# Gated linear attention and a bilinear feed-forward layer on one core: weight columns 256 to 768 in four transfers instead of two, GpSimd's scaling of k behind a gate, and products of chunk 1 ahead of chunk 2's last scores

## The chip, the cores and the metric

The kernel runs on one core of a Trainium2 chip. The metric is the device time of one execution in microseconds (us). For the kernel before there are three runs: 195.4, 194.96 and 194.41 us, median 194.96. One further execution, 195.32 us, was profiled; the profile's rows come from it, counted from the start of its span of 193.5 us. Its TensorE clock was granted in full throughout.

## The reference

Two layers stand behind each other. The first is a gated linear attention over 4 batches, 8 heads, 768 steps and a head size of 48; the second multiplies two linear maps of its output and maps the product back:

```python
for t in range(S):
    state = alpha[:, :, t, :, None] * state + einsum('bhd,bhe->bhde', k[:, :, t], v[:, :, t])
    y[:, :, t] = einsum('bhd,bhde->bhe', q[:, :, t], state)
x = y.transpose(0, 2, 1, 3).reshape(B * S, H * D)      # 3072 x 384
out = ((x @ w_a) * (x @ w_b)) @ w_out                  # 384 -> 1536 -> 384
```

All inputs and the output are float32.

## The kernel before

The work is cut into six chunks, 0 to 5. A chunk has two batches (called u = 0 and 1) and 256 steps, which are 512 tokens of the feed-forward layer. Even chunks have batches 0 and 1, odd ones batches 2 and 3; chunks 0 and 1 are the first third of the sequence, 2 and 3 the second, 4 and 5 the last.

The attention of a chunk is done in blocks. The logarithms of alpha (`ln`, ScalarE, L418) are summed along the steps by TensorE (`B`, `A2`, `AQ`), for which VectorE, GpSimd or ScalarE first prepare pairs and the parts of their values (`l2`, `lx`, `H`, `L`, `R`, L426 to L495). The exponentials of the sums (`E`, L539) scale k and q (`mk`, `mq`, VectorE, L550). Before that, the even steps of k and q are scaled by a single step's alpha or its inverse (`lv`, L524, on VectorE or GpSimd, 128x384 each). The scaled values are transposed, in chunks 0 and 1 by TensorE with a copy out of PSUM (`C` L591, `Ce` L597 or L599), later by a DMA transpose that SyncE issues (`T`, L602). Then come the scores (`D`, L672), which are masked on the way out of PSUM (`M` on VectorE, L677) or copied out by ScalarE and masked in place by VectorE (`Mc` L681, `Mm` L685). The output gathers a product with the carried state that crosses blocks (`SB`), one within (`SA`, both L696 or L701) and the product of masked scores and values (`Y`, L696 or L722). The new state is `K` or `KA` on TensorE (L625) and `k` on VectorE (L657 to L661). `X` copies the result out of PSUM (L762, L764), and from chunk 2 on a DMA transpose (`XT`, L769, issued by SyncE) turns it.

The feed-forward layer of a chunk has 12 blocks f of 128 columns of w_a and w_b. `a f w i` and `b f w i` (L784) are three matmuls of 128 rows into PSUM bank i; w is 0 or 1 for one batch (256 tokens) or * for both (512). `as` copies an `a` product into SBUF on ScalarE (L790), where three buffers serve in turn, and `pr` multiplies it on VectorE with the `b` product in PSUM (L798). `o m half i` (L806) is half of an output tile of 128 tokens, six matmuls of 384 columns; `ot` copies it out (L821, L823) and `st` stores it.

PSUM has eight banks. Each operation that writes PSUM names its bank as its last number; scores and `AQ`, `SB` take the named bank and the next one. A bank or a buffer is written again only when its last reader is done, and every wait of this kind is made by semaphores.

The order of all of it is written out by hand in the text PROGRAM (L17 to L265), one operation after the other as `chunk: operation arguments`. Each engine takes the instructions that fall to it in that order and never passes over one that waits. A letter at an operation's end names its engine: V VectorE, P GpSimd, S ScalarE, Y SyncE. DMA issues stand in their engine's order as well: `ld` loads a, q, k or v of a chunk (L411), `W a lo hi` columns lo to hi of w_a (L391, always issued by GpSimd, which turns float32 into bf16 on the way), `Wo` rows of w_out (L394). GpSimd's loads have eight semaphores in turn, so one is issued only when the eighth before it has landed.

The lines of PROGRAM around the change are these (`...` for what is left out):

```
0: W a 256 768; W b 256 768
...
0: SB 1 1; a 2 0 3; a 5 0 6; a 3 0 7; as 3 0; a 4 0 4; as 4 0; as 5 0; b 4 0 0; b 3 0 7
...
2: D 0 0 5; Mc 0 0; Mm 0 0 V; SB 0 1; SA 1; Y 1; X 1 S; XT 1
1: a 4 1 7
```

`gate_t` (L856) is a copy of one element of a transposed tile on GpSimd: GpSimd's later work is behind it, and it waits for the tile.

Of the kernel before, what the change touches and what calls it, by code (L numbers as in the profile page):

```python
# [20 lines left out]
0: cm 1; ld v 1 P; c2 P; c3 P; D 0 1 5; M 0 1; D 0 0 0; SB 0 6; B 1a 4; Bs 1a; Mc 0 0; Mm 0 0 V; B 1b 5; Bs 1b; E 1a i; E 1a b; mq 1a V; mk 1a V; K 0 1 4; E 1b i  # L21
0: v 1 V; mk 1b V; E 1b b; mq 1b V; SA 0; Y 0; X 0 S; dk 1 0; C 1 0 3; Ce 1 0 V; k 0 1 V; b 1 0 6; W a 0 256; de 1; K 1 0 5; k 1 0 V
1: ld a 1 P
0: W a 256 768; W b 256 768
1: ld a 0 P
0: W a 768 1536; C 1 1 1; a 1 0 2; as 1 0; pr 1 0; Ce 1 1 V; W b 768 1536
1: ld q 0 P; ln 1
0: b 0 0 4; a 0 0 2; as 0 0; pr 0 0; D 1 0 6; D 1 1 0; M 1 1
1: ld k 0 P; l2 1 P; ld v 0 P; ld k 1 P
0: Mc 1 0; Mm 1 0 V  # L30
1: H 1 S
0: SB 1 1; a 2 0 3; a 5 0 6; a 3 0 7; as 3 0; a 4 0 4; as 4 0; as 5 0; b 4 0 0; b 3 0 7
1: L 1 V
0: pr 4 0; pr 3 0; SA 1; Y 1; X 1 V; b 2 0 0
1: A2 1 7; ld q 1 P
0: Wo 0 6
2: ld a * P
0: K 1 1 5
1: ln 0
0: as 2 0; pr 2 0  # L40
1: l2 0 V; E 1 b; E 1 i; H 0 S
0: a 3 1 4; a 5 1 2; k 1 1 V; as 3 1; b 3 1 0; a 4 1 1; b 5 0 7; pr 5 0; as 5 1; a 6 * 5; b 5 1 4; a 11 * 3; pr 5 1; pr 3 1; as 4 1; b 4 1 1; pr 4 1
1: L 0 V; dk * 6
0: Wo 6 12; as 11 *; as 6 *
1: ra 0
0: b 6 * 3; pr 6 *; b 11 * 0; pr 11 *
1: A2 0 7; E 0 i; de *
2: ld q * P
1: lv 0 q P; ld v 1 P; lv 0 k V; mk 0 V
0: a 10 * 2; a 7 * 3  # L50
1: E 0 b; mq 0 V
0: as 10 *; a 2 1 4; as 2 1; b 10 * 1; pr 10 *; as 7 *; b 7 * 0; pr 7 *
1: v 0 S; ra 1
0: b 2 1 3; a 0 1 5
1: C 0 0 4
0: a 1 1 6; as 1 1
1: Ce 0 0 S
0: pr 2 1; b 1 1 1; pr 1 1; as 0 1
1: KA 0 02; k 0 0 V; k 0 1 V; C 0 1 7
0: b 0 1 6  # L60
1: Ce 0 1 S
2: ld k * P
1: lv 1 k P
3: ld a * P
0: pr 0 1
1: mk 1 V; lv 1 q P; mq 1 V
0: a 8 * 1; as 8 *; a 9 * 5; as 9 *
2: ld v * P
0: b 8 * 2; pr 8 *
1: D 0 0 6; M 0 0; D 0 1 3; Mc 0 1; SB 0 4  # L70
# [25 lines left out]
1: as 3 0; b 3 0 7; a 1 0 6; as 1 0  # L96
4: ld a * P
1: b 7 0 0; b 1 0 4; pr 1 0; as 7 0; pr 7 0; pr 3 0
2: mk 0 V
1: SB 1 0  # L100
3: ln *
1: a 6 0 2; as 6 0; b 9 0 3; a 4 0 5; a 9 0 6; as 9 0; pr 9 0
2: mq 1 V; T 1
0: o 2 0 4
1: b 4 0 6; b 6 0 7
2: lv 0 q P; mq 0 V
# [162 lines left out]
def kernel(  # L269
# [29 lines left out]
    ld = ctx.enter_context(tc.tile_pool(name="ld", bufs=2))  # L299
# [21 lines left out]
    go = cst.tile([1, 1], F32, name="go")  # L321
# [641 lines left out]
```

## Time and profile before

| | us |
|---|---|
| runs | 195.4, 194.96, 194.41 |
| median | 194.96 |
| profiled execution | 195.32 |
| its span | 193.5 |
| TensorE busy (matmuls) | 184.7 |
| VectorE busy | 138.4 |
| ScalarE busy | 103.3 |
| GpSimd busy | 50.8 |

Engines are named PE (TensorE matmul), PEld (its weight loads, beside the matmuls), DVE (VectorE), ACT (ScalarE), POOL (GpSimd) and SP (SyncE). A row of the timeline has the start and the length in us, the engine, the line of the kernel, the operation, the written and the read tile, their shapes, a count where equal instructions were merged, and in brackets the idle time before it with what ended it. Matmuls overlap, so that a row's length is more than the distance to the next one, and the distance is what a step costs. In the view by slices a digit is the busy share of a fortieth of the span in tenths. A row of the DMA view has the transfer, the queue, the count, the size in SBUF and the time from issue to landing.

### The profile page before, as it was taken

The page shows a single profiled execution, that of the slowest core. Times are in us where ns is not written, and L with a number is a line of the kernel's source. Part 1 is how long each engine was busy: PE and PEld are TensorE (multiplying, and loading weights), DVE is VectorE, ACT ScalarE, POOL GpSimd, SP SyncE. Part 2 cuts the span into 40 slices and gives each one's busy share as a digit, 9 for nine tenths or more (in the row PEclk, how much of TensorE's full clock was granted, in tenths as well). Part 3 has the DMA queues.
Part 4 walks back from the last instruction along what each step waited for, and adds up shares of the span by engine and source line. Part 5 has one row for each costly group of instructions (what it writes and reads, how often), then busy time and mean ns, then how long its engine had stood idle before and what let it go on. Part 6 is the DMA issues. An engine that isn't in the chain of part 4 may idle for free.

```text
span 193.5 us, 5877 instructions
## 1 busy us (share of the span) xinstructions
PE 184.7 (95%) x2509; PEld 111.4 (58%) x2509; DVE 138.4 (71%) x230; ACT 103.3 (53%) x189; POOL 50.8 (26%) x71
## 2 busy tenths in 40 slices
PE   7889699999999998999999999999999999999993
PEld 3467475666687865744556644555544566544462
DVE  4688777999899799597979499875854871156520
ACT  4565575886775676556565235875255622154401
POOL 8999645850640425000400020050000000000000
PEclk9999999999999999999999999999999999999999
DMA  5999999999999999489995488999297005021013
GB/s 139 261 214 211 243 247 251 252 246 260 243 220 231 198 234 219 57 233 213 172 219 69 100 203 178 118 191 120 59 180 160 3 3 122 0 99 67 0 42 122
DMA packets 67162, 30.96 MB, mean 160 GB/s; under 512 B 58064, under 2 KB 65120, under 8 KB 67136
## 3 DMA queue, kind: packets, MB, share of 16 engines
q0 software_dynamic: 18640, 14.16, 41.3%
q1 hardware_dynamic: 48352, 16.34, 39.9%
q8 instruction: 19, 0.31, 0.7%
q10 hardware_dynamic: 144, 0.10, 0.2%
q14 instruction: 7, 0.06, 0.1%
HBM read 25.98 MB, written 4.74 MB: 159 GB/s over the span
## 4 chain that ended last, share of the span: by engine, by line
PE 84%; POOL 6%; DMA 5%; issue 2%; DVE 1%; ACT 0%; POOLq 0%; DVEq 0%
PE psum L784 47%; PE psum L806 24%; DMA wb_t<-in_moe_w_b_dram 5%; PE psum L672 3%; PE psum L722 2%; PE psum L625 2%; PE psum L696 2%; PE psum L701 1%; PE psum L505 1%; PE psum L817 1%; POOL v_t L411 1%; POOL a_t L411 1%; PE psum L591 1%; POOL wa_t L391 1%; DVE prod L798 1%
## 5 line engine op out<-in xcount | busy, mean ns | idle before, releaser
L784 PE MATMUL psum<-xT,wb_t 128*128 128x512 bf16 (+1 forms) x270 | 57.0, 337 | 1.3 <-DMA wb_t<-in_moe_w_b_dram 1.3
L784 PE MATMUL psum<-xT,wa_t 128*128 128x512 bf16 (+1 forms) x270 | 56.1, 337 | 0.0
L806 PE MATMUL psum<-wo_t,prod 128*128 128x384 bf16 x276 | 48.5, 326 | 0.0
L784 PEld LDWEIGHTS <-wb_t 128*128 128x128 bf16 x270 | 25.5, 98 | 21.9 <-DMA wb_t<-in_moe_w_b_dram 1.6
L784 PEld LDWEIGHTS <-wa_t 128*128 128x128 bf16 x270 | 25.6, 98 | 19.7 <-issue 0.2
L806 PEld LDWEIGHTS <-prod 128*128 128x128 bf16 x276 | 26.1, 98 | 17.0
L681 ACT ACTIVATE m<-psum 128x1024 bf16<-128x1024 f32 x16 | 16.3, 1023 | 6.1 <-PE psum L672 5.9
L823 DVE COPY ot<-psum 128x384 f32<-128x384 f32 (+1 forms) x13 | 6.9, 538 | 15.7 <-PE psum L806 13.2
L524 POOL TENSOR_TENSOR q_t<-q_t,ra 128x384 f32<-128x384 f32 x8 | 8.8, 1103 | 34.7 <-DVE prod L798 18.4
L821 ACT ACTIVATE ot<-psum 128x384 f32<-128x384 f32 (+1 forms) x12 | 5.7, 477 | 12.9 <-PE psum L806 11.9
L524 POOL TENSOR_TENSOR k_t<-k_t,a_t 128x384 f32<-128x384 f32 x5 | 6.0, 1197 | 22.8 <-DVE QKp L550 17.9
L685 DVE TENSOR_TENSOR m<-m,mask 128x1024 bf16<-128x1024 bf16 x16 | 11.6, 734 | 0.3 <-ACT m L681 0.2
L418 ACT ACTIVATE la<-a_t 128x1536 f32<-128x1536 f32 (+2 forms) x9 | 9.5, 1053 | 3.7 <-DMA a_t<-in_alpha_dram 3.7
L550 DVE TENSOR_TENSOR QKp<-k_t,invb 128x768 bf16<-128x768 f32 x10 | 11.0, 1105 | 0.2
L677 DVE TENSOR_TENSOR m<-psum,mask 128x1024 bf16<-128x1024 f32 x8 | 9.8, 1219 | 1.6 <-PE psum L672 1.5
L550 DVE TENSOR_TENSOR QKp<-q_t,beta 128x768 bf16<-128x768 f32 x10 | 9.3, 947 | 0.0
L672 PE MATMUL psum<-kqT 64*64 64x128 bf16 x384 | 8.6, 218 | 0.2 <-DVE kqT L599 0.2
L411 POOL DMA_DIRECT2D v_t<-in_v_dram x8 | 8.6, 1075 | 0.6 <-PE psum L784 0.5
L762 ACT ACTIVATE ys<-psum 128x768 bf16<-128x768 f32 x7 | 5.6, 808 | 5.6 <-PE psum L722 3.3
L672 PEld LDWEIGHTS <-kqT 64*64 64x64 bf16 x384 | 6.3, 107 | 2.7 <-issue 2.3
L411 POOL DMA_DIRECT2D a_t<-in_alpha_dram x6 | 6.3, 1043 | 5.6 <-DVE prod L798 2.9
L444 PE MATMUL psum<-wz 128*128 128x512 bf16 x17 | 5.5, 473 | 1.2 <-DVE og L336 1.2
(272 smaller groups left out, 272.0 us busy)
## 6 DMA issues: line engine op xcount, KB each, us to landing
out_dram<-ot SPq DMA_DIRECT2D x23, 192.0 KB, 2.6
a_t<-in_alpha_dram POOLq DMA_DIRECT2D x3, 768.0 KB, 14.2
k_t<-in_k_dram SPq DMA_DIRECT2D x3, 768.0 KB, 6.7
q_t<-in_q_dram POOLq DMA_DIRECT2D x2, 768.0 KB, 12.8
v_t<-in_v_dram POOLq DMA_DIRECT2D x4, 384.0 KB, 9.2
q_t<-in_q_dram SPq DMA_DIRECT2D x2, 768.0 KB, 6.7
a_t<-in_alpha_dram POOLq DMA_DIRECT2D x3, 384.0 KB, 5.7
q_t<-in_q_dram POOLq DMA_DIRECT2D x3, 384.0 KB, 13.1
```

The lines of the kernel that those rows point to most:

```text
L411: eng.dma_start(out=t[:, us, hs].rearrange("p b h r d -> p (b h) (r d)"), in_=src[ch.b0 + us.start:ch.b0 + us.stop, hs, ch.s * 2 * C:(ch.s ...
L418: nc.scalar.activation(out=ch.la[:, us, hs].rearrange("p b h r d -> p (b h r d)"), in_=ch.a[:, us, hs].rearrange("p b h r d -> p (b h r d) ...
L524: eng.tensor_mul(x, x, by)
L550: eng.tensor_mul(QKp[ch.c % 2][:, u, j, :, hs, :D], src[:, u, hs].rearrange("p h r d -> p r h d"), f)
L672: nc.tensor.matmul(s2[g * HC:(g + 1) * HC, r, p, rk, :], lhsT=ch.kqT[u][rs, 1, rk, 2 * h + p, g * HC:(g + 1) * HC], rhs=queriesT(ch, u, 2 ...
L677: nc.vector.tensor_mul(m.rearrange("p r a k s -> p (r a) (k s)"), ch.s2[u, h].rearrange("p r a k s -> p (r a) (k s)"), maskn(4))
L681: nc.scalar.activation(out=m.rearrange("p r a k s -> p (r a) (k s)"), in_=ch.s2[u, h].rearrange("p r a k s -> p (r a) (k s)"), func=AF.Copy)
L685: eng.tensor_mul(x, x, maskn(4))
L784: nc.tensor.matmul(p, lhsT=(wa_t, wb_t)[w][:, kk, f * 128:(f + 1) * 128], rhs=ch.xT[:, us.start // 2:us.stop // 2, kk].rearrange("p u g s ...
L806: nc.tensor.matmul(op, lhsT=ch.prod[:, f, at:at + C], rhs=wo_t[:, f, :], start=(f == 0), stop=(f == NFF - 1))
L821: nc.scalar.activation(out=o_, in_=i_, func=AF.Copy)
L823: eng.tensor_copy(o_, i_)
```

## The change

It has four parts, all but one of them moves of operations in PROGRAM. The number of matmuls and their shapes stay the same.

1. The loads of columns 256 to 768 of w_a and w_b, two transfers of 512 columns each, become four of 256 columns, in the order a, b, a, b. Behind them the products of chunk 0 are put in another order: `b 2` and `b 3` come before `a 4` and `a 5`, and `b 4` and `b 5` behind chunk 0's inner products. `SB 1` stands ahead of the second half of the scores. `H` and `L` come behind the `as` copies. Many PSUM banks are other ones.
2. In chunk 1, GpSimd's scaling `lv 0 q` stands ahead of the load of chunk 2's q instead of behind it, `lv 1 k` and `lv 1 q` ahead of the load of chunk 3's alpha. `a 10` goes ahead of the products that need the last columns of w_b; `a 1 1` ahead of the transposes `C 0 0`; `pr 7` ahead of `pr 10`.
3. In chunk 2, `mq 1` and the transpose `T 1` stand ahead of `mk 0`. Chunk 1's `a 4 1`, `as 4 1` and `o 0 0` stand ahead of chunk 2's last scores `D 0 0`, and `o 0 1` directly behind its `Y 1`; `b 9 1` comes behind `AQ 3`.
4. GpSimd's scaling of chunk 3's k (`lv 0 k`, `lv 1 k`) moves behind a new `gatem 0 0`, a copy of one element of chunk 2's last masked scores.

```diff
-0: W a 256 768; W b 256 768
+0: W a 256 512; W b 256 512; W a 512 768; W b 512 768
...
-0: b 0 0 4; a 0 0 2; as 0 0; pr 0 0; D 1 0 6; D 1 1 0; M 1 1
+0: b 0 0 4; a 0 0 2; as 0 0; pr 0 0; D 1 0 6; SB 1 2; D 1 1 0; M 1 1
...
-1: H 1 S
-0: SB 1 1; a 2 0 3; a 5 0 6; a 3 0 7; as 3 0; a 4 0 4; as 4 0; as 5 0; b 4 0 0; b 3 0 7
-1: L 1 V
-0: pr 4 0; pr 3 0; SA 1; Y 1; X 1 V; b 2 0 0
+0: a 2 0 4; as 2 0; a 3 0 5; as 3 0; b 2 0 6; pr 2 0; b 3 0 0; a 4 0 7; as 4 0; a 5 0 1; as 5 0; pr 3 0
+1: H 1 S; L 1 V
+0: SA 1; Y 1; X 1 V; b 4 0 4; pr 4 0; b 5 0 5; pr 5 0
...
-0: a 3 1 4; a 5 1 2; k 1 1 V; as 3 1; b 3 1 0; a 4 1 1; b 5 0 7; pr 5 0; as 5 1; a 6 * 5; b 5 1 4; a 11 * 3; pr 5 1; pr 3 1; as 4 1; b 4 1 1; pr 4 1
-1: L 0 V; dk * 6
+0: a 3 1 1; a 5 1 2; k 1 1 V; as 3 1; b 3 1 0; a 4 1 3; as 5 1; b 5 1 4; as 4 1; b 4 1 5; pr 3 1; pr 5 1; a 6 * 6; a 11 * 7; pr 4 1
+1: L 0 V; dk * 1
+0: a 10 * 2
...
+1: lv 0 q P
 2: ld q * P
-1: lv 0 q P; ld v 1 P; lv 0 k V; mk 0 V
-0: a 10 * 2; a 7 * 3
+1: ld v 1 P; lv 0 k V; mk 0 V
+0: a 7 * 4
...
-0: as 10 *; a 2 1 4; as 2 1; b 10 * 1; pr 10 *; as 7 *; b 7 * 0; pr 7 *
+0: as 10 *; a 2 1 5; as 2 1; b 10 * 1; as 7 *; b 7 * 0; pr 7 *; pr 10 *
...
-1: KA 0 02; k 0 0 V; k 0 1 V; C 0 1 7
+1: KA 0 02; k 0 0 V; k 0 1 V; C 0 1 1
...
-3: ld a * P
...
+3: ld a * P
-0: a 8 * 1; as 8 *; a 9 * 5; as 9 *
+0: a 8 * 7; as 8 *; a 9 * 5; as 9 *
...
-2: mk 0 V
+2: mq 1 V; T 1
...
-2: mq 1 V; T 1
+2: mk 0 V
...
-3: ra 1; lv 1 q P; ld v * P; lv 0 k P; lv 1 k P
+3: ra 1; lv 1 q P; ld v * P
...
-2: D 0 0 5; Mc 0 0; Mm 0 0 V; SB 0 1; SA 1; Y 1; X 1 S; XT 1
-1: a 4 1 7
+1: a 4 1 5; as 4 1; o 0 0 7
+2: D 0 0 1; Mc 0 0; Mm 0 0 V; gatem 0 0; SB 0 5; SA 1; Y 1; X 1 S; XT 1
+3: lv 0 k P; lv 1 k P
+1: o 0 1 -; ot 0 V
 4: ln *
-1: as 4 1; b 9 1 0; pr 9 1; o 0 0 5
 3: AQ 3
+1: b 9 1 0; pr 9 1
 2: SA 0; Y 0; X 0 S; XT 0
 5: ld a * Y
-1: o 0 1 -; ot 0 V; a 1 1 6; a 10 1 1; as 1 1; as 10 1
+1: a 1 1 1; a 10 1 2; as 1 1; as 10 1
...
+    def gate_m(x, u, h):
+        nc.gpsimd.tensor_copy(go, x.m[int(u), int(h)][0:1, 0, 0, 0, 0:1])
```

More of the change, by code (lines that the diff above doesn't have):

```diff
@@ L37 @@
 2: ld a * P
-0: K 1 1 5
+0: K 1 1 6
 1: ln 0
-0: as 2 0; pr 2 0
 1: l2 0 V; E 1 b; E 1 i; H 0 S
-0: a 3 1 4; a 5 1 2; k 1 1 V; as 3 1; b 3 1 0; a 4 1 1; b 5 0 7; pr 5 0; as 5 1; a 6 * 5; b 5 1 4; a 11 * 3; pr 5 1; pr 3 1; as 4 1; b 4 1 1; pr 4 1
-1: L 0 V; dk * 6
+0: a 3 1 1; a 5 1 2; k 1 1 V; as 3 1; b 3 1 0; a 4 1 3; as 5 1; b 5 1 4; as 4 1; b 4 1 5; pr 3 1; pr 5 1; a 6 * 6; a 11 * 7; pr 4 1
+1: L 0 V; dk * 1
+0: a 10 * 2
 0: Wo 6 12; as 11 *; as 6 *
@@ L47 @@
 1: A2 0 7; E 0 i; de *
+1: lv 0 q P
 2: ld q * P
-1: lv 0 q P; ld v 1 P; lv 0 k V; mk 0 V
-0: a 10 * 2; a 7 * 3
+1: ld v 1 P; lv 0 k V; mk 0 V
+0: a 7 * 4
 1: E 0 b; mq 0 V
-0: as 10 *; a 2 1 4; as 2 1; b 10 * 1; pr 10 *; as 7 *; b 7 * 0; pr 7 *
+0: as 10 *; a 2 1 5; as 2 1; b 10 * 1; as 7 *; b 7 * 0; pr 7 *; pr 10 *
 1: v 0 S; ra 1
-0: b 2 1 3; a 0 1 5
-1: C 0 0 4
-0: a 1 1 6; as 1 1
+0: b 2 1 3; a 0 1 6; a 1 1 4
+1: C 0 0 5
+0: as 1 1
 1: Ce 0 0 S
-0: pr 2 1; b 1 1 1; pr 1 1; as 0 1
-1: KA 0 02; k 0 0 V; k 0 1 V; C 0 1 7
-0: b 0 1 6
+0: pr 2 1; b 1 1 7; pr 1 1; as 0 1
+1: KA 0 02; k 0 0 V; k 0 1 V; C 0 1 1
+0: b 0 1 4
 1: Ce 0 1 S
@@ L127 @@
 2: Mm 1 0 V
-1: o 2 0 7
+1: o 2 0 6
 2: SB 1 3; D 0 1 1; Mc 0 1; Mm 0 1 V; k * 1 V
@@ L133 @@
 1: st 2 Y
-2: D 0 0 5; Mc 0 0; Mm 0 0 V; SB 0 1; SA 1; Y 1; X 1 S; XT 1
-1: a 4 1 7
+1: a 4 1 5; as 4 1; o 0 0 7
+2: D 0 0 1; Mc 0 0; Mm 0 0 V; gatem 0 0; SB 0 5; SA 1; Y 1; X 1 S; XT 1
+3: lv 0 k P; lv 1 k P
+1: o 0 1 -; ot 0 V
 4: ln *
-1: as 4 1; b 9 1 0; pr 9 1; o 0 0 5
 3: AQ 3
+1: b 9 1 0; pr 9 1
 2: SA 0; Y 0; X 0 S; XT 0
 5: ld a * Y
-1: o 0 1 -; ot 0 V; a 1 1 6; a 10 1 1; as 1 1; as 10 1
+1: a 1 1 1; a 10 1 2; as 1 1; as 10 1
 3: E 0 b; E 0 i
-1: b 4 1 2; pr 4 1; b 8 1 5; b 1 1 1; a 8 1 6; b 10 1 0; pr 1 1; o 3 0 2; pr 10 1; as 8 1; pr 8 1; o 3 1 -; ot 3 S; st 3 Y
+1: b 4 1 7; pr 4 1; b 8 1 0; b 1 1 5; a 8 1 6; b 10 1 1; pr 1 1; o 3 0 2; pr 10 1; as 8 1; pr 8 1; o 3 1 -; ot 3 S; st 3 Y
 2: a 4 * 7; as 4 *
@@ L861 @@
         "gatet": gate_t,
+        "gatem": gate_m,
         "c1": lambda x: const_fill(),
```

## The prediction

> **What bounds the kernel now.** I read the page first, then the timeline of TensorE for its waits, and only around these the other engines.
>
> ```profile
> PE 184.7 (95%) x2509; PEld 111.4 (58%) x2509; DVE 138.4 (71%) x230; ACT 103.3 (53%) x189; POOL 50.8 (26%) x71
> DMA  5999999999999999489995488999297005021013
> ```
>
> TensorE is busy 95% of the span, and the DMA engines are full from slice 2 to 16, so to about 78 us. The change leaves every matmul in place, so only idle TensorE time can be won. Its timeline shows two waits of over a microsecond behind the start-up (in brackets: the idle time and what ended it). The first is in chunk 0, with three later points that I use below:
>
> ```profile
> 23.40 0.83 PE L784 MATMUL psum<-xT,wb_t 128*128 128x256 bf16 x6 [1.30 <-DMA wb_t<-in_moe_w_b_dram]
> ...
> 27.91 0.81 PE L784 MATMUL psum<-xT,wa_t 128*128 128x512 bf16 x3
> ...
> 37.59 0.44 PE L625 MATMUL psum<-vx,QKp 64*64 64x48 bf16 x32
> ...
> 40.78 0.64 PE L672 MATMUL psum<-kqT 64*64 64x128 bf16 x32
> ```
>
> At 23.40 `b 4 0` waits for columns 256 to 768 of w_b. 27.91 is `a 6`, the first product that needs columns from 768 on; 37.59 is `KA 0` and 40.78 `D 0 0` of chunk 1. The second wait is in chunk 2:
>
> ```profile
> 71.70 0.42 PE L672 MATMUL psum<-kqT 64*64 64x128 bf16 x16
> ...
> 73.50 0.18 PE L701 MATMUL psum<-S,kqT 64*64 64x48 bf16 x1 [1.26 <-issue]
> ...
> 74.25 0.50 PE L784 MATMUL psum<-xT,wa_t 128*128 128x256 bf16 x3
> ...
> 74.92 1.14 PE L806 MATMUL psum<-wo_t,prod 128*128 128x384 bf16 x6
> ...
> 77.24 1.15 PE L806 MATMUL psum<-wo_t,prod 128*128 128x384 bf16 x6
> ...
> 82.50 1.46 PE L784 MATMUL psum<-xT,wa_t 128*128 128x512 bf16 x6
> ```
>
> These rows are `D 0 0`, `SA 1`, `a 4 1` (with `b 9 1` behind it), `o 0 0`, `o 0 1`, and chunk 2's first product `a 4 *`. The view calls the cause of the 1.26 us "issue"; the VectorE rows show it:
>
> ```profile
> 70.01 0.95 DVE L495 TENSOR_TENSOR lh<-l 128x768 f32<-128x768 f32 x1
> 70.88 0.68 DVE L685 TENSOR_TENSOR m<-m,mask 128x1024 bf16<-128x1024 bf16 x1
> ...
> 72.99 0.56 DVE L661 TENSOR_TENSOR S<-tmp,bl 128x384 bf16<-128x384 f32 x1
> 73.46 1.76 DVE L495 TENSOR_TENSOR ll<-lh 128x768 f32<-128x768 f32 x1
> 75.14 1.49 DVE L685 TENSOR_TENSOR m<-m,mask 128x1024 bf16<-128x1024 bf16 x1
> 73.24 2.84 POOL L524 TENSOR_TENSOR k_t<-k_t,a_t 128x384 f32<-128x384 f32 x2 [4.47 <-DMA k_t<-in_k_dram]
> ```
>
> `SA 1` reads the state that L661 finishes at 73.55. The last row is GpSimd's scaling of chunk 3's k: beside it L495 takes 1.76 us and L685 1.49, where the first two rows, of the same forms, took 0.95 and 0.68.
>
> **Part 1: products ahead of chunk 2's scores.** Two 256-wide products lie between 74.25 and 74.92, so one is 0.33 us. From 77.24 to 82.50 run three halves of `o` and seven products: (5.26 - 7 x 0.33) / 3 = 0.98 for a half. The change puts `a 4 1` and `o 0 0` ahead of `D 0 0`: 0.33 + 0.98 = 1.31 us. `D 0 0` then starts near 73.0, and its own 0.24 and the state products reach the wait at about 73.5, when the state is ready. So the wait is filled, and as nothing but the order changed, everything behind `Y 1` has 1.31 us less ahead of it. The DVE row that releases `SA 1` keeps its place. I count 1.25, the wait itself.
>
> What is late next is chunk 2's transposed activations, `XT 0`, which `a 4 *` needs:
>
> ```profile
> 77.35 0.81 ACT L762 ACTIVATE ys<-psum 128x768 bf16<-128x768 f32 x1 [0.54 <-PE psum L722]
> xT<-ys SPq DMA_TRANSPOSE x8, 3.1
> kqT<-QKp SPq DMA_TRANSPOSE x8, 4.4
> ```
>
> Now the copy ends at 78.16 and the transpose lands 3.1 us on, at 81.3, against 82.50. Changed, `a 4 1` (0.33) no longer lies between `Y 1` and `Y 0`, so the copy ends near 77.8 and the landing is at 80.9, against `a 4 *` at 82.50 - 1.25 = 81.25. It is still covered, by 0.35. At 4.4 us (the median of the other kind of transpose) it would be 82.2, a new wait of 0.95; if it lands sooner, nothing is gained. I take 0, as 3.1 is of the same kind.
>
> The `gatem` copy holds GpSimd until chunk 2's last mask product is done. VectorE's L495 and L685 then run at 0.95 and 0.68, so 1.6 us of VectorE time come free, but `Y 0`, which reads L685's result, stands behind `o 0 1`, the cumulative sums and `b 9 1` anyway: 0. Queued behind the gate on GpSimd are the two scalings of k (at most 1.42 each, done by about 78) and then chunk 4's q; chunk 3's `mk 0`, which waits for them, stands behind `a 4 *`, so after 81. The copy itself is one element. Also 0; were this cover gone, it would be 2.84. Swapping `mq 1` and `mk 0` of chunk 2 lets SP issue its first transpose one product of VectorE (0.95) earlier, ahead of the same queue: 0.
>
> **Part 2: four weight transfers.** The queue is first in, first out, so landing is issue plus the view's last figure. First the GpSimd rows of the issues, then the landings, each with its own issue:
>
> ```profile
> 12.74 0.92 POOL L411 DMA_DIRECT2D a_t<-in_alpha_dram  x1
> 13.65 0.75 POOL L391 DMA_DIRECT2D wa_t<-in_moe_w_a_dram  x1
> 14.38 0.76 POOL L391 DMA_DIRECT2D wb_t<-in_moe_w_b_dram  x1
> ...
> 16.01 0.80 POOL L391 DMA_DIRECT2D wa_t<-in_moe_w_a_dram  x1
> ...
> 18.42 0.92 POOL L411 DMA_DIRECT2D k_t<-in_k_dram  x1
> ```
>
> ```profile
> a_t<-in_alpha_dram POOLq DMA_DIRECT2D x1, 384.0 KB, 5.7
> wa_t<-in_moe_w_a_dram POOLq DMA_DIRECT2D x1, 384.0 KB, 6.6
> wb_t<-in_moe_w_b_dram POOLq DMA_DIRECT2D x1, 384.0 KB, 9.0
> wa_t<-in_moe_w_a_dram POOLq DMA_DIRECT2D x1, 576.0 KB, 11.2
> k_t<-in_k_dram POOLq DMA_DIRECT2D x1, 384.0 KB, 14.7
> ```
>
> So alpha lands at 18.4, w_a's middle at 20.25, w_b's at 23.4, w_a's last part at 27.2, chunk 1's k at 33.1. The two middle transfers take 1.8 and 3.1, together 4.9. Cut in four, b 2 and b 3 have their columns near 20.3, and a 4, a 5 near 21.8. The two issues more (0.76 each) delay GpSimd by 1.5 us, and its `l2 1` behind them, but every load behind them waits 5 us or more in the queue anyway.
>
> How much later the four land as a whole, d, no row shows. A half at the faster transfer's rate is 0.9, at the slower's 1.57; four are 3.6 or 6.3 against 4.9: d between -1.3 and +1.3. I take +0.4: each has rows half as long, which can hardly be quicker, while w_a's last part and the alpha ahead of it, 960 KB from 23.4 to 27.2, or 0.76 per 192 KB, speak for a price by the byte.
>
> The Trainium skill (DMA: Bandwidth & Descriptors, Measured (HBM→SBUF, 128 partitions, SWDGE, issued from GpSimd)) speaks against cutting: batch to 1 MiB; its 0.95 us for 64 KB and 6.15 for 1 MB leave, as an estimate, 0.6 fixed for each transfer. By it d is 1.2 and the sum below 1.0 instead of 1.8.
>
> **What TensorE does with it.** Two more rows, from VectorE's timeline and from the chain of work that ended last:
>
> ```profile
> 20.47 1.23 DVE L677 TENSOR_TENSOR m<-psum,mask 128x1024 bf16<-128x1024 f32 x1 [0.17 <-PE psum L672]
> 24.23 0.95 PE psum L696 x54
> ```
>
> TensorE ran dry at 22.1 (23.40 - 1.30) after four products (`a 2` to `a 5`, 1.32). Now `a 2`, `a 3`, `b 2` come first, 0.33 each. `b 3` writes bank 0, which `M 1 1` (the L677 row) empties at 21.7, and 0.27 later as `SB 1` now stands ahead of its scores: a wait of up to 0.4. Then `b 3`, `a 4`, `a 5` (0.99) and the 54 inner matmuls (0.95) bring it to 23.9, and `b 4` needs 23.4 + 0.4 = 23.8. So 1.30 - 0.4 = 0.9 is in hand. At `a 6` TensorE has 0.66 more behind it (`b 4 1`, `b 5 1`): 27.91 + 0.66 - 0.9 = 27.7, and its columns land at 27.2 + 0.4 = 27.6. But it is not all kept, because chunk 1 hangs on k's landing:
>
> ```profile
> 33.18 0.56 DVE L524 TENSOR_TENSOR k_t<-k_t,a_t 128x384 f32<-128x384 f32 x1
> 33.84 1.57 DVE L550 TENSOR_TENSOR QKp<-k_t,invb 128x768 bf16<-128x768 f32 x1
> 35.33 0.95 DVE L550 TENSOR_TENSOR QKp<-q_t,beta 128x768 bf16<-128x768 f32 x1
> 36.20 0.72 DVE L798 TENSOR_TENSOR prod<-as__705,psum 128x512 bf16<-128x512 bf16 x1
> 33.26 1.33 POOL L524 TENSOR_TENSOR q_t<-q_t,ra 128x384 f32<-128x384 f32 x1
> 37.10 0.38 ACT L790 ACTIVATE as__741<-psum 128x256 bf16<-128x256 f32 x1 [0.82 <-PE psum L784]
> 39.59 0.60 ACT L790 ACTIVATE as__812<-psum 128x512 bf16<-128x512 f32 x1
> ```
>
> L524 starts as k lands. GpSimd's q scaling, which stretches `mk 0` to 1.57, moves ahead of a load that GpSimd issues, to about 32 to 33, so `mk 0` takes 0.95. With d = 0.4: k at 33.5, then about 0.55 + 0.9 + 0.9 to 35.85, then `pr 7` and `pr 10` at 0.62 each, now in this order, to 37.1. `KA 0`, released by `pr 7`, starts at 36.5 instead of 37.59. But `as 1 1` takes the buffer that `pr 10` gives back, so ScalarE's row at 37.10 stays there, and so its chain to the row at 39.59 (`as 8`, done 40.2). `a 8` now sits in bank 7, which `D 0 0` needs: 40.2 instead of 40.78. The head is worth 0.55: with d = +1.3 it is a loss of 0.35; with d = -1.3 the products' own time caps it, I estimate at the 1.1 that `KA 0` wins.
>
> **The sum.** 1.25 + 0.55 = 1.8 us. The profiled execution took 195.32, its span 193.5 and 1.8 around it, so its span should be 191.7. That execution is 0.36 above the median of the runs, 194.96; from the median the time is 193.2, and with the bounds of d alone, 0.9 to 2.35 less, 192.6 to 194.1.
>
> **The rivals.** First, the landings eat the head (d of 1 or more): only 1.25 less something is left, 193.7 to 194.1. The full DMA slices speak for it, the price by the byte against it. The skill's page says the same, in d = 1.2. Chance 0.17.
>
> Second, the wait moves to `XT`: at 4.4 us, 0.95 goes back, 194.1 to 194.2. For it speaks that only 0.35 covers it; against, that DMA traffic falls off in just these slices. 0.10.
>
> Third, the order doesn't do what it says: the state at 73.55 comes later as well, since VectorE's row waits for a mask on ScalarE, or the head's stalls only move. Nothing in the rows delays it; 195.0. 0.06.
>
> Fourth, the slower end: a transfer's price goes by the piece. Four at the mean of the two, 2.47, are 9.9 against 4.9, d = 4.9: k lands at 38.0, `D 0 0` comes at 44.7, 3.9 late, and with 1.25 won 2.7 are lost: 197.7. It decides against the change from d = 2.2 on. The 0.76 per 192 KB speaks against it. 0.12.
>
> **How the numbers follow.** The forecast holds 0.55. Within 0.5% (about what a measurement of this kernel can tell from no change) is 194.0 to 195.9. Faster: 0.53 of the forecast, 0.10 of the first rival, 0.02 of the second: 0.65. Slower: the fourth and a little else, 0.13. The rest, 0.22, is the same. The range, 192.2 to 195.1, takes the forecast with 0.4 of scatter below it, the three middle rivals, and leaves out the fourth.
>
> **What would show it.** Right: no wait for wb_t near 23, or one under 0.4; `SA 1` without its 1.26; L495 near 0.95 and the following L685 near 0.68; w_a's last part landing by 28; `a 4 *` about 1.8 us earlier. Wrong: w_a's last part landing after 28.5, a new wait at `a 6` or `D 0 0` of chunk 1 above 1 us, or TensorE waiting at `a 4 *` for the transpose.

## The result, and the profile after

| | before | after |
|---|---|---|
| median of 8 runs, us | 195.23 | 196.82 |
| lowest to highest | 194.41 to 195.64 | 195.69 to 198.33 |
| profiled execution | 195.32 | 196.17 |
| its span | 193.5 | 194.4 |

The ratio of the two times is 1.0077, with a 95% interval of 1.0051 to 1.0103: the changed kernel is slower by 0.8%. Here and below, ratios are estimated from the runs outside a slower state of the chip, and are not exactly the quotients of the medians, which have all runs. The line numbers of the helpers are two further down than before, and in the experiments up to six.

First comes the timeline of TensorE after the change, at the places that the prediction spoke of (start, length, engine, line, operation, tiles, shape, count, and the idle time before it with what ended it):

```profile
16.08 0.43 PE L627 MATMUL psum<-vx,QKp 64*64 64x48 bf16 x16 [0.76 <-ACT prod L541]
...
23.33 0.49 PE L786 MATMUL psum<-xT,wb_t 128*128 128x256 bf16 x3 [0.23 <-DVE m L679]
...
40.77 0.64 PE L674 MATMUL psum<-kqT 64*64 64x128 bf16 x32
...
67.49 0.64 PE L674 MATMUL psum<-kqT 64*64 64x128 bf16 x32 [0.46 <-DMA kqT<-QKp]
...
77.58 0.50 PE L786 MATMUL psum<-xT,wa_t 128*128 128x256 bf16 x3
79.39 0.50 PE L786 MATMUL psum<-xT,wa_t 128*128 128x256 bf16 x3 [1.31 <-issue]
...
83.31 1.46 PE L786 MATMUL psum<-xT,wa_t 128*128 128x512 bf16 x6
```

The wait for w_b's columns at 23.4 is gone, and so are the 1.26 us at `SA 1`. But `D 0 0` of chunk 1 stands at 40.77, where it was before (40.78), `D 1 1` of chunk 2 at 67.49 instead of 66.97 (its row of before is the one below), behind a wait for `T 1` that was not there, and `a 10 1` at 79.39 behind a new wait of 1.31. `a 4 *` comes at 83.31, 0.81 later than before, and this distance stays to the end: the spans differ by 0.9.

```profile
66.97 0.64 PE L672 MATMUL psum<-kqT 64*64 64x128 bf16 x32
```

Part of the lost start belongs to this one execution. Its clock row on the page, and the row of before for the first line above:

```profile
PEclk9969999999999999999999999999999999999999
```

```profile
14.49 0.43 PE L625 MATMUL psum<-vx,QKp 64*64 64x48 bf16 x16 [0.58 <-ACT prod L539]
```

The third slice, from 9.7 to 14.6 us, was granted 0.6 of the clock, and TensorE was 1.6 us behind at 16 us, ahead of anything that the change touches; before had the full clock throughout. The other runs after were nearly all at full clock and not faster, so the dip is not why the kernel is slower; it hides what the head would have shown here.

The late `D 1 1` has its counterpart in SyncE's queue. Its timeline (SPq: issues of DMA), after and then before:

```profile
57.50 0.54 SPq L841 DMA_DIRECT2D out_dram<-ot  x1
58.95 8.32 SPq L604 DMA_TRANSPOSE kqT<-QKp  x2
```

```profile
57.55 0.53 SPq L839 DMA_DIRECT2D out_dram<-ot  x1
60.15 6.08 SPq L602 DMA_TRANSPOSE kqT<-QKp  x2
```

`T 1` and `T 0` of chunk 2 were issued 1.2 us earlier, and the issue took 2.2 us longer. By its semaphore `T 1` landed at 67.44 instead of 65.97: **issued earlier, landed later.**

VectorE and GpSimd did what was forecast:

```profile
73.98 0.95 DVE L497 TENSOR_TENSOR ll<-lh 128x768 f32<-128x768 f32 x1
75.04 0.69 DVE L687 TENSOR_TENSOR m<-m,mask 128x1024 bf16<-128x1024 bf16 x1
```

```profile
75.96 1.96 POOL L526 TENSOR_TENSOR k_t<-k_t,a_t 128x384 f32<-128x384 f32 x2
```

With the scaling behind the gate, L497 takes 0.95 instead of 1.76 and L687 0.69 instead of 1.49. And the transfers, from GpSimd's issues and from the DMA view (last figure: median from issue to landing):

```profile
17.83 0.74 POOL L393 DMA_DIRECT2D wa_t<-in_moe_w_a_dram  x1
```

```profile
wb_t<-in_moe_w_b_dram POOLq DMA_DIRECT2D x3, 192.0 KB, 6.2
wa_t<-in_moe_w_a_dram POOLq DMA_DIRECT2D x1, 576.0 KB, 9.7
```

w_a's last part lands at 17.83 + 9.7 = 27.5, against 27.2 before, and chunk 1's k by its semaphore at 33.43 against 33.09: what stands behind the four transfers comes 0.3 to 0.4 us later, about as assumed. The four themselves land, by their semaphores, at 19.36, 20.34, 21.33 and 22.39, so the last of them is even 1.0 ahead of w_b's transfer before (23.35); the alpha behind them lands at 25.03 instead of 24.61. In another run with the four transfers, e1 below, they land at 19.69, 21.11, 23.16 and 23.71, so the time of a single one scatters.

**What "issue" is.** The instruction that stops at 79.39, `a 10 1`'s first weight load, has no semaphore to wait for, and neither had the product of `SA 1` that stopped before; each only follows the products ahead of it. The page shows one queue that the prediction passed over:

```profile
q8 instruction: 19, 0.31, 0.7%
```

These are 19 packets, 0.31 MB, so 16 KB each, spread over the whole span: TensorE's own code on its way to it. They serve 5018 weight loads and matmuls (2509 each on the page), one packet for some 264. Counting TensorE's instructions in the trace in order of their start (its few semaphore instructions too), the stop at `SA 1` before stands behind number 2241 and the one at `a 10 1` after behind number 2497: exactly 256 apart, or 64 bytes of a packet for each. And the stop ends 1.64 us after the end of such a packet (70.70 to 71.86, stop over at 73.50), after the change 1.48 us (76.98 to 77.91, over at 79.39). So theory CODE was that TensorE runs into a block of 256 instructions that has not come yet; where hundreds of short matmuls follow each other, it uses a block up faster than the next one comes.

### The profile page after: what moved, and what is told of

Its sections match the earlier page's. It is cut to its first block, busy times and chain, and to the rows that moved or that the text cites. A ratio compares the mean times of both kernels' runs of the same rounds, so it can differ in the third digit from the quotient of the medians.

```text
span 194.4 us, 5878 instructions
## 1 busy us (share of the span) xinstructions
PE 185.7 (96%) x2509; PEld 112.6 (58%) x2509; DVE 135.8 (70%) x230; ACT 103.2 (53%) x189; POOL 51.7 (27%) x74
## 4 chain that ended last, share of the span: by engine, by line
PE 86%; DMA 7%; DVE 2%; SPq 1%; issue 1%; ACT 1%; DVEq 0%
PE psum L786 45%; PE psum L808 23%; DMA kqT<-QKp 4%; PE psum L674 3%; DMA k_t<-in_k_dram 2%; PE psum L627 2%; PE psum L724 2%; PE psum L698 2%; PE psum L593 2%; PE psum L703 1%; PE psum L507 1%; SPq L413 1%; PE psum L819 1%; PE psum L573 1%; PE psum L462 1%
## 5 line engine op out<-in xcount | busy, mean ns | idle before, releaser
L687 DVE TENSOR_TENSOR m<-m,mask 128x1024 bf16<-128x1024 bf16 x16 | 10.8, 686 | 0.4 <-ACT m L683 0.3
L526 POOL TENSOR_TENSOR k_t<-k_t,a_t 128x384 f32<-128x384 f32 x5 | 5.4, 1085 | 18.4 <-DVE QKp L552 17.5
L552 DVE TENSOR_TENSOR QKp<-q_t,beta 128x768 bf16<-128x768 f32 x10 | 9.8, 988 | 0.0
L552 DVE TENSOR_TENSOR QKp<-k_t,invb 128x768 bf16<-128x768 f32 x10 | 9.5, 951 | 0.2
L674 PE MATMUL psum<-kqT 64*64 64x128 bf16 x384 | 9.2, 226 | 0.5 <-DMA kqT<-QKp 0.5
```

Source lines behind the costliest of these rows:

```text
L526: eng.tensor_mul(x, x, by)
L552: eng.tensor_mul(QKp[ch.c % 2][:, u, j, :, hs, :D], src[:, u, hs].rearrange("p h r d -> p r h d"), f)
L674: nc.tensor.matmul(s2[g * HC:(g + 1) * HC, r, p, rk, :], lhsT=ch.kqT[u][rs, 1, rk, 2 * h + p, g * HC:(g + 1) * HC], rhs=queriesT(ch, u, 2 ...
L687: eng.tensor_mul(x, x, maskn(4))
```

## The experiments

Names of theories: CODE as above. TRANSPOSE: the swap of `mq 1; T 1` with `mk 0` makes `T 1` late, and that is the loss. HEAD: the four transfers cost the time. Each ratio is against the kernel before, measured beside it on the same chip (medians 195.4 to 195.5, and 195.23 for the first comparison), with its 95% interval.

### The parts one by one

Four kernels: the new head alone (parts 1 and 2 of the change), the swap alone, the new order in chunk 2 with the gate alone, and the changed kernel without the swap.

```diff
 e1: before +
-0: W a 256 768; W b 256 768
+0: W a 256 512; W b 256 512; W a 512 768; W b 512 768
...
 e2: before +
+2: mq 1 V; T 1
...
-2: mq 1 V; T 1
+2: mk 0 V
 e3: before +
+1: a 4 1 5; as 4 1; o 0 0 7
+2: D 0 0 1; Mc 0 0; Mm 0 0 V; gatem 0 0; SB 0 5; SA 1; Y 1; X 1 S; XT 1
...
 e4: after, with the lines of e2 undone
```

> The kernel before with the change's first part alone (the four weight transfers and the new order of products in chunk 0); chunk 2's order is the old one. Theory CODE (TensorE stops where it reaches a stretch of 256 of its instructions that has not been fetched yet; the change only moved that stop from `SA 1` to `a 10 1`) and theory TRANSPOSE (the earlier `T 1` lands later, `D 1 1` of chunk 2 waits for it): both say that the head does nothing, as chunk 1's `KA 0` and `D 0 0` started at the same times in both profiles: within 0.4 us of the kernel before, the 1.26 us stop at `SA 1` still there. Theory HEAD (the loss comes from the four transfers): slower by 0.8 us or more, with `D 0 0` of chunk 1 after 41.3.

> The kernel before with one move alone: `mq 1; T 1` ahead of `mk 0` in chunk 2. TRANSPOSE: `T 1` is issued about 1.2 us earlier and lands 1 to 1.5 us later, `D 1 1` starts 0.5 us later, the time is 0.4 to 0.8 us more. CODE: a later `D 1 1` comes ahead of the stop at `SA 1`, whose end is set by the fetch and not by TensorE, so 0 to 0.3 us more and a shorter stop. My prediction's own step said 0.

> The kernel before with the last part alone: `a 4 1`, `o 0 0` ahead of chunk 2's `D 0 0`, the GpSimd gate, no swap, old head. CODE: no stop at `SA 1`, one of 1.2 to 1.6 us 256 instructions later, before `a 10 1`; `a 4 *` within 0.4 us of the kernel before, and so is the time. TRANSPOSE and HEAD: the wait at `SA 1` is filled and stays filled, 1.0 to 1.25 us less.

> The changed kernel with the swap undone (`mk 0` ahead of `mq 1; T 1` again), all else as changed. TRANSPOSE: it wins back 0.5 to 1.6 us against the changed kernel and comes out at or below the kernel before. CODE: the stop before `a 10 1` stays at 1.2 to 1.9 us; at most 0.5 us is won back against the changed kernel. HEAD: still 0.8 us or more slower than before.

| | median, us | ratio to before |
|---|---|---|
| e1, head alone | 194.59 | 0.9962 (0.9944 to 0.9981) |
| e2, swap alone | 195.79 | 1.0019 (0.9991 to 1.0047) |
| e3, order and gate alone | 195.60 | 1.0006 (0.9983 to 1.0028) |
| e4, after without swap | 195.30 | 1.0017 (0.9989 to 1.0046) |
| after | 196.82 | 1.0077 (1.0051 to 1.0103) |

HEAD falls: the head wins 0.4%, where CODE and TRANSPOSE had expected nothing and HEAD a loss. One row of e1's TensorE shows it, `D 0 0` of chunk 1 at 40.22 instead of 40.78:

```profile
40.22 0.64 PE L672 MATMUL psum<-kqT 64*64 64x128 bf16 x32
```

The order in chunk 2, which was to win 1.25 us, wins nothing, and its stop is where CODE put it. From the timelines of e3, then of e4:

```profile
78.13 0.60 PE L786 MATMUL psum<-xT,wa_t 128*128 128x256 bf16 x4 [0.69 <-issue]
...
82.32 1.47 PE L786 MATMUL psum<-xT,wa_t 128*128 128x512 bf16 x6
```

```profile
78.54 0.50 PE L786 MATMUL psum<-xT,wa_t 128*128 128x256 bf16 x3 [1.28 <-issue]
...
82.47 1.46 PE L786 MATMUL psum<-xT,wa_t 128*128 128x512 bf16 x6
```

In both `SA 1` does not wait, `a 10 1` does, and `a 4 *` is at 82.3 and 82.5 as before (82.50). In e1 and e2, where the order is the old one, the stops stand at the same two counts, 2241 and 2497, in other shares (e1: none and 0.76, although the one at `SA 1` was expected to stay; e2: 0.48 and 1.08), since the fetch comes earlier or later in every run. The swap alone costs nothing that can be told, and yet the changed kernel is 0.6% above e4 by their ratios (1.5 us by the medians). That is what TRANSPOSE had expected of e4; CODE had allowed 0.5 us at most. The parts do not add up, and the next runs look for the reason.

### Moving the boundaries

The same work, with more TensorE instructions ahead of it: the warm-up products at the start, whose result nobody reads, are cut into pieces of 64 columns. Every boundary of 256 then falls on another instruction. From the profile before, the time that TensorE needs for each block of 256 at any shift is read off as the distance of two starts, less the stops.

```diff
 e5: before +                      (16 instructions more)
-fill 7 2
+fill 6 2; fine 9 2
 e6: before +, e7: e4 +, e8: after +   (210 more)
-fill 7 2 ... fill 9 2
+fine 56 2 ... fill 1 2; fine 64 2
+    def fine(n, i):
+        for _ in range(n):
+            nc.tensor.matmul(bank(i)[:, :64], lhsT=wz[:, :C], rhs=wz[:, :64], start=True, stop=True)
```

> The kernel before with one warm-up product of 512 columns at the start cut into smaller ones, so that 16 more TensorE instructions lie ahead of everything else, over no more columns than before plus 64; nothing else. CODE: every stretch of 256 ends 16 instructions earlier in the work; from the profile of before the stretch ahead of the second boundary in chunk 2 then holds 3.9 us of work instead of 4.9, so a second stop appears there beside that at `SA 1`: 0.6 to 1.1 us slower. TRANSPOSE and HEAD: same within 0.3 us.

> The kernel before with the warm-up products at the start cut into pieces of 64 columns: 210 more TensorE instructions over the same columns, which puts each boundary where it would stand with 46 fewer. CODE: the stretches of chunk 2 then hold 4.6 and about 7.5 us of work: one stop of about 1.0 us ahead of the scores' end instead of 1.45 plus what is short behind it, 0.4 to 0.9 us faster, unless a new stop near 18 us, where a stretch of 4.9 us now stands in the start-up, takes it back. TRANSPOSE and HEAD: same within 0.3 us.

> The changed kernel with the swap undone and the warm-up products cut into pieces of 64 columns (210 more TensorE instructions over the same columns). CODE: the stretches of chunk 2 hold 5.8 and 6.5 us of work, so neither `SA 1` nor `a 10 1` stops by more than 0.3: 1.2 to 1.7 us faster than without the extra instructions, 193.6 to 194.1, below the kernel before. TRANSPOSE and HEAD: as without them, 195.3 within 0.3.

> The changed kernel as it is, with the warm-up products cut into pieces of 64 columns (210 more TensorE instructions over the same columns). CODE: the stop before `a 10 1` is gone or under 0.3 and the kernel 1.2 to 1.7 us faster than the changed one; what the swap costs by itself (`D 1 1` of chunk 2 waiting for `T 1`, 0.46 us) is what is left between this kernel and the one without the swap. TRANSPOSE: D 1 1's wait is the whole loss, so still 196 or more.

| | median, us | ratio to before |
|---|---|---|
| e5, before + 16 | 197.44 | 1.0086 (1.0054 to 1.0118) |
| e6, before + 210 | 195.22 | 0.9989 (0.9959 to 1.0020) |
| e7, e4 + 210 | 193.99 | 0.9933 (0.9909 to 0.9958) |
| e8, after + 210 | 196.53 | 1.0057 (1.0023 to 1.0090) |

In e5 eight small matmuls at the start, some 190 us ahead of the end, make the kernel slower by 0.9%, and its timeline has two stops where before had one:

```profile
72.91 0.18 PE L705 MATMUL psum<-Sm,kqT 64*64 64x48 bf16 x1 [0.67 <-issue]
...
77.73 1.14 PE L810 MATMUL psum<-wo_t,prod 128*128 128x384 bf16 x6 [0.61 <-issue]
```

The median rose by 2.0 (1.7 by the ratio), where CODE said 0.6 to 1.1; these two rows, 1.28 together, don't hold more than the one of before (1.26), `a 4 *` comes 0.47 later than before, and the profiled execution (195.85) is the fastest of its eleven. So the sign and the second stop are shown; what the slower executions lost is not. e6 keeps the one stop that was expected (0.96), but isn't shown to be faster: 0.4 to 0.9 us were expected, and its interval includes none. e7 is as expected: no stop, and 193.99, below both kernels. What it gains is seen in the view of busy time by stretch, from 58 to 83 us, for before, after and e7 (length, then the busy time of PE, PEld, DVE, ACT and POOL with their instructions, clock, DMA, GB/s):

```profile
58.00:83.00 25.00, 23.74 (x464) 17.69 (x463) 21.10 (x37) 15.03 (x31) 6.33 (x6) 1.00 1.04 189
```

```profile
58.00:83.00 25.00, 23.23 (x460) 17.00 (x459) 18.98 (x36) 14.68 (x30) 5.61 (x7) 1.00 1.13 199
```

```profile
58.00:83.00 25.00, 25.00 (x469) 18.05 (x468) 20.83 (x39) 15.95 (x33) 5.56 (x6) 1.00 1.14 206
```

Before, TensorE stood for 1.26 in these 25 us, after for 1.77, in e7 not at all, and `a 4 *` is at 81.16. That is 1.34 earlier than before, of which 0.15 were there at `D 0 0` of chunk 1 (40.63), so some 1.2 of the order's 1.25 are won.

e8 refutes that the new stop alone made the changed kernel slow. CODE expected it 1.2 to 1.7 us faster than the changed kernel; it stays above 196, as TRANSPOSE had said. It has no stop either, but two other waits:

```profile
67.64 0.64 PE L678 MATMUL psum<-kqT 64*64 64x128 bf16 x32 [1.41 <-DMA kqT<-QKp]
...
83.26 1.47 PE L790 MATMUL psum<-xT,wa_t 128*128 128x512 bf16 x6 [1.04 <-DMA xT<-ys]
```

The first is `D 1 1` behind `T 1`, the second `a 4 *` behind `XT`; e7, the same kernel but for the swap, has neither, and is 2.5 us faster. So in these two kernels the swap does cost time, and why is the next question.

### Why the earlier transpose lands later

The packets of `T 1` and `T 0` (256 bytes each) start near 61.5 us in every profile, whenever they were issued, and go at full rate, about 280 in a quarter of a microsecond, from 64 on. In the profiles with the swap there is a hole of 1.0 to 1.5 us in them, behind a 16 KB packet of TensorE's code. COLLISION says that the code packet halts the transpose; ISSUE ORDER that an earlier issue is itself slower.

```diff
 e9: after +                       (112 instructions more)
-fill 7 2 ... fill 9 2
+fine 56 2 ... fill 8 2; fine 8 2
 e10: before +                     (192 more)
+fine 56 2 ... fill 2 2; fine 54 2
 e13: after +                      (96 more)
+fine 55 2 ... fill 9 2
 e14: before +                     (160 more)
+fine 56 2 ... fill 5 2; fine 35 2
```

> The changed kernel with 112 more TensorE instructions at the start (warm-up products cut into pieces of 64 columns): TensorE now enters a new stretch of 256 near 56.7 us and the next near 66.5 us, none near 60. Theory COLLISION (the earlier `T 1` gets ahead of TensorE's fetch, which then falls into the middle of `T 1`'s packets and halts all of them for 1.5 us): no fetch between 61 and 66 us, no hole in the packets of `T 1`, which lands by 66.2 instead of 67.4; `D 1 1` of chunk 2 waits under 0.2 and starts by 67.0. Theory ISSUE ORDER (an earlier issue itself makes `T 1` land later): it still lands at 67 or later and `D 1 1` waits 0.4 or more. Either way CODE expects a stop of 1 to 2 us near 70 to 76 us, as the stretch from 66.5 holds 4.2 us of work, so the time is no better than the changed kernel's by more than 0.8 us.

> The kernel before, no swap, with 192 more TensorE instructions at the start (same columns, smaller pieces): TensorE enters a new stretch near 62.1 us, after SP has issued `T 1` at about 60.1. COLLISION: the fetch starts at 64 or later, in the middle of `T 1`'s packets; `T 1` lands at 67 or later though nothing was swapped, and `D 1 1` of chunk 2 waits 0.3 us or more. ISSUE ORDER: `T 1` lands at 66.0 as before and nothing waits.

> The changed kernel, swap and all, with 96 more TensorE instructions at the start (same columns, smaller pieces), which puts boundaries of 256 near 57.3 and 67.7 us. COLLISION: the first's fetch starts by 62 us, ahead of the full run of `T 1`'s packets, and the second's behind them; no hole in the packets, `T 1` lands by 66.6 although it was issued near 58, and `D 1 1` of chunk 2 waits under 0.3. ISSUE ORDER: `T 1` lands at 67.2 or later again, as in all four profiles with the swap so far. CODE: a stop of 1 us or more follows near 71, as the stretch from 67.7 holds 3.3 us of work.

> The kernel before, no swap, with 160 more TensorE instructions at the start (same columns, smaller pieces), which puts boundaries of 256 near 54.2 and 63.7 us. COLLISION: a fetch starts between 63.8 and 65.8 us, in the full run of `T 1`'s packets; a hole of about 1.3 us in them, `T 1` lands at 67 or later though issued near 60, and `D 1 1` of chunk 2 waits 0.4 us or more. ISSUE ORDER: no swap, so `T 1` lands between 65.9 and 66.8 as in all ten profiles without it.

e9 and e10 missed, as the fetches were not where they had been worked out: e9's came at 65.74, still within `T 1`, and e10's at 61.79, ahead of it. (e9: 198.24 from four runs, ratio 1.0131, 1.0082 to 1.0179; e10: 195.47, ratio 0.9990, 0.9957 to 1.0023.) e13 and e14 hit in what they say of `T 1`: with the swap and the fetch behind `T 1`, `T 1` lands at 66.11; without the swap and with the fetch in it, at 67.25. Their rows for `D 1 1`, e13 first:

```profile
66.16 0.64 PE L678 MATMUL psum<-kqT 64*64 64x128 bf16 x32
```

```profile
67.30 0.64 PE L676 MATMUL psum<-kqT 64*64 64x128 bf16 x32 [0.69 <-DMA kqT<-QKp]
```

CODE missed in e9 and in e13. The stop of 1 us or more that it expected there between 70 and 76 us did not come. The packet that was to be late started just as TensorE entered the short stretch (e13: 66.20, entry at 66.23; e9: 65.74, entry at 65.52), and only e13 lost 0.29 at the boundary after it. e9 instead stood 2.07 us at `D 1 1`, and 1.65 at a boundary much later, until 106.71. So where a stop can fall is told by the count; whether it comes, and how long it is, hangs on when the packet comes, and that was not foretold well.

All 16 profiles, from the DMA packets and semaphores of their traces (us; hole: quarters of a microsecond with under 100 of the transposes' packets, once they run at full rate):

```
                 T 1 issued   code packet starts   T 1 lands   hole
no swap
before               60.15        62.24              65.97      none
e1                   59.92        62.61              66.60      none
e3                   60.15        62.04              65.96      none
e4                   59.86        61.81              66.38      none
e5                   60.22        61.74              65.97      none
e6                   60.11        61.99              66.10      none
e7                   60.01        62.50              66.52      none
e10                  59.88        61.79              66.22      none
e11                  60.31        62.43              66.80      none
e12                  60.14        62.06              66.09      none
e14                  59.72        65.02              67.25      65.75 to 67.00
swap
after                58.95        64.44              67.44      65.00 to 66.25
e2                   59.17        64.27              67.24      64.75 to 66.25
e8                   58.17        64.69              67.60      65.25 to 66.50
e9                   57.90        65.74              67.93      66.50 to 67.50
e13                  57.98        66.20              66.11      66.75 to 68.25 (in T 0)
```

ISSUE ORDER falls with e13 and e14; COLLISION holds in all 16. The hole begins 0.3 to 0.6 us after the start of the one code packet, which takes 1.05 to 1.2 us, and ends 0.8 to 0.9 after its end; meanwhile 17 to 21 packets of the transposes are on their way for over a microsecond (up to 1.46 in after, 1.64 in e13), and the others stand. Ahead of 64 us the transposes' packets come slowly anyway, and no hole of its own can be told there.

The code packets also touch `XT 0`, the transpose that `a 4 *` needs. The semaphore of a transpose counts 16 parts. In e4, e8, e12 and after, 15 parts of `XT 0` land together and the last one 1.6 to 1.9 us later, 1.1 to 1.3 behind the end of a code packet (after: 81.27 and 83.14, packet from 81.06 to 81.99; e4: 80.48 and 82.36, packet from 80.00 to 81.09). In e3 a packet from 79.19 to 80.55 leaves a hole in `XT 0`'s packets, and all of it lands at 82.28. In e7 it has landed at 80.62, ahead of the packet at 80.84. So in e3, e4 and after, `a 4 *` (82.32, 82.47 and 83.31) starts only 0.04 to 0.17 us after `XT 0` is there. Without the stop before `a 10 1` it could hardly have come earlier, as e8 shows, where it waits for `XT 0` (landed at 83.21); and e7, which wins over e4, has neither the stop nor a packet in `XT 0`. No run tried this by itself, and in e1, e6 and e11 a packet starts as close ahead of the landing without making the last part late.

e13's median is 195.03 (ratio 0.9976, 0.9936 to 1.0016): the changed kernel, swap and all, comes out 1% better for 96 instructions at the start, though not shown to be below the kernel before. e14's is 195.42 (0.9985, 0.9959 to 1.0011). In e14's timeline the stop at the boundary bears another name:

```profile
74.45 0.49 PE L788 MATMUL psum<-xT,wa_t 128*128 128x256 bf16 x3 [1.26 <-ACT ys L766]
```

Its count is 2497 and it ends 1.36 after a code packet. The row is `a 4 1`, and in before the same product started at 74.25, ahead of the same copy (74.36 to 75.17), so ScalarE's copy was not what was waited for. These are all stops at boundaries over 0.25 us from 68 to 82 us:

```
         behind no.   stop             code packet ended   stop over later by
before     2241     72.05 to 73.50         71.86               1.64
after      2497     77.81 to 79.39         77.91               1.48
e1         2497     77.17 to 77.93         76.44               1.49
e2         2241     72.36 to 72.84         71.48               1.36
e2         2497     77.68 to 78.76         77.54               1.22
e3         2497     77.17 to 78.13         76.46               1.67
e4         2497     76.99 to 78.54         77.29               1.25
e5         2241     72.05 to 72.91         71.29               1.62
e5         2497     77.06 to 77.73         76.44               1.29
e6         2496     72.33 to 73.47         71.97               1.50
e10        2496     72.20 to 72.74         71.06               1.68
e12        2241     72.06 to 73.31         71.77               1.54
e12        2497     78.26 to 78.68         77.25               1.43
e13        2497     75.80 to 76.09         74.69               1.40
e14        2497     73.12 to 74.45         73.09               1.36
```

### The gate and the four transfers

```diff
 e11: e7, without the gate
-3: ra 1; lv 1 q P; ld v * P
+3: ra 1; lv 1 q P; ld v * P; lv 0 k P; lv 1 k P
...
-2: D 0 0 1; Mc 0 0; Mm 0 0 V; gatem 0 0; SB 0 5; SA 1; Y 1; X 1 S; XT 1
-3: lv 0 k P; lv 1 k P
+2: D 0 0 1; Mc 0 0; Mm 0 0 V; SB 0 5; SA 1; Y 1; X 1 S; XT 1
 e12: e1, with two transfers
-0: W a 256 512; W b 256 512; W a 512 768; W b 512 768
+0: W a 256 768; W b 256 768
```

> The changed kernel with the swap undone, 210 more TensorE instructions at the start, and without the gate: chunk 3's two scalings of k go to GpSimd where they stood before. All theories, and the prediction's own step: VectorE's masks take 1.7 and 1.5 us again instead of 0.95 and 0.69, but TensorE does not wait for them, so the same time as with the gate within 0.4 us (194.0). If the gate matters, 0.5 to 1.5 us slower, with a wait of TensorE for the masked scores near 75 us.

> The kernel before with the new order of chunk 0's products, but columns 256 to 768 of each weight still in one transfer (two transfers instead of four). If the four transfers are what the head wins by (my prediction's step): TensorE waits 0.7 us or more for w_b's columns near 22 to 23 us and most of the 0.7 us (194.6 against 195.4) that the head with four transfers wins is gone: 195.0 to 195.6. If the order alone wins it: 194.6 within 0.3.

e11 took 194.03 (ratio 0.9939, 0.9908 to 0.9970) against 193.99 for e7: the gate is worth nothing that can be told, as said. e12 took 197.17 (1.0063, 1.0023 to 1.0103), more than was expected: the new order of products without the four transfers loses 0.6%, and with them it wins 0.4%, so the transfers are worth 1% to the head, some 2 us. Its TensorE waits at the same place as before, a little longer:

```profile
23.11 0.83 PE L784 MATMUL psum<-xT,wb_t 128*128 128x256 bf16 x6 [1.45 <-DMA wb_t<-in_moe_w_b_dram]
```

This execution took 195.56, near the lowest of its twelve; what the others lost no profile shows.

## Why the prediction was wrong

**Part 1, the 1.25 us, failed at its cause.** The step was "`SA 1` reads the state that L661 finishes at 73.55": the state and the stop ended within 0.05 us of each other, and the view's word "issue" was put aside for a row that fitted. It did not even fit quite: `SA 1` went on at 73.50, 0.05 ahead of L661's end. The wait was for TensorE's code. In every run with the new order `SA 1` is free, as forecast, but a block of 256 instructions that used to hold `a 4 1` and `o 0 0` now lacks them, TensorE is through it in 4.0 us (73.80 to 77.81), and the next block comes 5.6 us after the last one was entered. The stop went one block on and was 1.58 instead of 1.45. Its sign "`SA 1` without its 1.26" came true and told nothing.

**The swap, "ahead of the same queue: 0", failed.** The queue was not the same: TensorE's code passes through the DMA engines too. In the changed kernel it met `T 1` at full rate and `D 1 1` waited; what the swap costs is 0.6% between e4 and after (1.2 us by the ratios), and 2.5 us between e7 and e8, where `XT` was late as well.

**Part 2 was right in sign and size, and partly by luck.** d was 0.3 to 0.4, about as taken. The Trainium skill's price (DMA: Bandwidth & Descriptors, Measured (HBM→SBUF, 128 partitions, SWDGE, issued from GpSimd)) gave 1.2 as an estimate; w_a's last part landing 0.3 to 0.4 later doesn't agree with it. `b 3` waits 0.23 for bank 0 (up to 0.4 was said). The head was put at 0.55: `D 0 0` of chunk 1 is 0.56 earlier in e1, whose time is 0.4% below that of before (0.7 us by the ratio). The way there was another one: `KA 0` was to come 1.1 earlier and half of that to be lost at the bank of `a 8`, but `KA 0` came 0.57 earlier (37.02) and `D 0 0` followed at the old distance of 3.2. Elsewhere `D 0 0` stands at 40.48 (e4), 40.63 (e7) and 39.98 (e8), so the 0.56 is one execution's. The profiled execution after shows none of it, behind a start that was 1.6 late.

**The zeros.** The gate: right (e11). `XT`: this zero failed too. It was to land 3.1 us after the copy and be covered by 0.35; in the changed kernel its last part landed 4.6 after the issue, behind a code packet, and no wait shows only because TensorE came 0.17 later still. In e8 `a 4 *` waits 1.04 for it. The second rival's 0.95 is near to that by luck: it took the whole transpose to be as slow as the other kind, and here 15 of 16 parts landed after 2.9. **The rivals:** none had the mechanism. The fourth, on the slower side, hung on d of 2.2 or more, which was 0.4. The third ("the head's stalls only move") came nearest, with the wrong stall.

The sum had 1.8 us less; in the profiled executions it was 0.85 more. Followed along TensorE these are 0.52 at `D 1 1`, 0.13 by which the new stop exceeds the old one (1.58 against 1.45 between two starts), and 0.2 in waits that are shorter than that. The medians differ by 1.59; the other 0.7, and the wide scatter of the runs after, are seen in no profile and stay open.

## What to carry to other kernels

A wait called "issue", or one whose named releaser was done long before, ought to be counted in instructions: if it falls on a multiple of 256 from the next such wait, and 1.2 to 1.7 us behind a packet of the instruction queue, suspect code that is late, which a reorder may only move. Shifting the boundaries can help: here 210 more instructions at the start turned a kernel without gain (195.3) into one of 193.99, 0.7% below before. It can also do nothing or harm, as e6, e5 and e9 show, so each shift has to be measured. Spreading long matmuls so that each block of 256 lasts longer than its fetch should help as well, but was not tried. And parts of a change that touch a stage with tight blocks should be tried together and apart, since their times don't add.

## What the runs showed of the hardware

- TensorE's code comes in 19 packets of 16 KB (20 in kernels with many more instructions), one for each block of 256; in none of the 16 profiles did a block's first instruction start sooner than 1.22 us after its packet's end. From entering a block to having the next took 5.6 and 5.9 us in the stops of after and before. The packets start 0 to 4.4 us after the entry in chunk 2's blocks. In before it is 2.6 us for the block entered at 94.59, where the page's DMA row has a 9, and 0.7 for the one entered at 106.02 (packet at 106.72), where it has a 5 and a 4.
- The Trainium skill (Runtime: NRT & Kernel Launch, Instruction fetch mechanics) says that instructions arrive in blocks of 16 KiB, 256 each, fetched while the current one runs, and that a crossing is "mostly hidden". The traces agree on the block and on its being fetched during the one before. Most of the 19 or 20 crossings of each profile are indeed hidden, but 15 of them in chunk 2 stood open for 0.29 to 1.58 us, and e9's at 106.71 for 1.65. It also gives TensorE room for 2048 instructions; no run here shows more than the next block fetched ahead of a stop.
- One code packet that meets a DMA transpose at full rate holds it up for 1.0 to 1.5 us, and the hole outlasts the packet by 0.8 to 0.9 us. Why the packet comes at 64.3 to 64.7 with the swap, 2 us later than without, was not tried: that it queues behind the transpose's packets is only argued.
